# Softmax blocks on VectorE in batches of three instead of two, and seven query chunks in the first of two layers

## The chip, the cores and the metric

The kernel runs on one core of one Trainium2 chip. The metric is the device time of one execution in microseconds (us). A core has five engines with instruction queues of their own: TensorE (PE in the profile, its weight loads PEld), VectorE (DVE), ScalarE (ACT), GpSimd (POOL) and SyncE (SP, which here issues DMAs). They run beside each other and meet at semaphores. SBUF is the on-chip memory; PSUM, eight banks of 512 fp32 columns, is where matmuls write.

## The reference

Two rounds of attention and a gated MLP over 2048 tokens of width 512, with the same weights in both rounds:

```python
x = A_x
x = x + _A_ref(_layernorm(x), A_wq, A_wk, A_wv, A_wo)
x = x + _B_ref(_layernorm(x), B_w_in, B_w_sp, B_b_sp, B_w_out)
x = x + _A_ref(_layernorm(x), A_wq, A_wk, A_wv, A_wo)
x = x + _B_ref(_layernorm(x), B_w_in, B_w_sp, B_b_sp, B_w_out)

def _A_ref(x, wq, wk, wv, wo):          # H = 32 heads of Dh = 16, one shared key and value head
    q = (x @ wq).reshape(B, S, H, Dh).transpose(0, 2, 1, 3)
    k, v = x @ wk, x @ wv
    scores = einsum('bhqd,bkd->bhqk', q, k) * Dh ** -0.5
    p = softmax(scores, axis=-1)
    return einsum('bhqk,bkd->bhqd', p, v).transpose(0, 2, 1, 3).reshape(B, S, H * Dh) @ wo

def _B_ref(x, w_in, w_sp, b_sp, w_out):
    z = gelu(x @ w_in)                  # 1792 wide, two halves of 896
    z1, z2 = z[..., :896], layernorm(z[..., 896:])
    g = einsum('ts,bsf->btf', w_sp, z2) + b_sp[None, :, None]   # mixes over all 2048 tokens
    return (z1 * g) @ w_out
```

The bulk of the work is the softmax: 2 layers x 32 heads x 2048 queries x 2048 keys are exponentiated.

## The kernel before

**Blocks, units, groups, chunks.** A *block* is the scores of 128 keys by 512 query columns, one PSUM bank. The keys are kept transposed in `kT`, in two masked versions `v`, with four copies of the key head on four row groups `j`; `qs` holds 128 rows (eight heads) of 512 query columns. One matmul of 32 rows (L1774, `_qk`) makes one block. Four blocks, one for each `j`, make a *unit* (one tile of 128 keys), and 16 units, all keys, make a *group*. Each layer has 32 groups, 512 units and 2048 blocks. Queries are cut into *chunks* (L441, `self.chunks`). For a chunk of 512 queries, the 512 columns are one set of eight heads; for one of 256, two sets stand side by side (`ns = 512 // n` in `layer_groups`), so a chunk of 256 needs only two token tiles of queries and takes four groups instead of eight. `make_q` (L808) makes the query columns.

**Exponentials.** `FillStream` fills five banks with scores, as a ring of three and a ring of two. `ExpStream` (L1434) lets ScalarE exponentiate three or two banks in one instruction into slots of `Pa` (15 slots of 512 columns). `DexStream` takes single blocks away from ScalarE and gives them to VectorE: such a block goes to a side bank of PSUM, and VectorE works it off without a table. L1626 scales it out of PSUM into fp32 `ey` (one instruction for each block). Then L1651, L1653, L1654, L1655 and L1657, each over a whole batch of `NDB` blocks, evaluate a polynomial in fp16 and add it into the bits of a bf16 number in slots of `Pd` (`NPD` slots). `LOOK` is how many units ahead of the filling such a block is picked. `PVStream` (L1517) multiplies the blocks of each unit, in order, by the values `V` (with a column of ones for the softmax sums), and so frees the slots.

**What follows a group and a chunk.** `finish_group` copies the sums out of PSUM (L841 to `oT`), transposes them (by DMA, or on PE near the end of a layer) and divides (L856, L868). After a chunk's last group, `project` multiplies by `wo` (L948) and adds to `X`, and `mixer_chunk` does the layer norm and the matmuls of `w_in` (L980 for z2, L1016 for z1). The gelu waits for a whole batch of chunks (`self.gelus`, L443), so that ScalarE changes its table of functions seldom. `spatial` (L1158, L1171, L1172) mixes over tokens for those tokens that are ready (`self.passes`, L442, names the chunk after which a pass may start), and `closing` does the last token tile, the product with z1 and `w_out` (L1217, L1228 to L1250).

**What sets the order.** Each engine runs a list that is fixed before the launch. A planner in the kernel (`Sched`) lays out all operations with assumed lengths and priorities, and writes for each engine its order with the semaphore waits it needs. So a changed constant moves work in every list. `WarmStream` (L1755) adds matmuls of a zero tile: where the planner sees fewer than `TICK_COLS + WARM` columns in 3.41 us, it puts one in, to keep PE's clock up; they compute nothing that is used.

**Loads at the start.** `load` fetches the eight parts of `A_x` and the weights, and sends `w_sp` through 16 DMA transposes into `gp` as staging (L597) and out to a scratch in HBM (L599). They share SP's queue with the transposes of the attention.

Of the kernel before, what the change touches and what calls it, by code (L numbers as in the profile page):

```python
# [370 lines left out]
E_A = 0.9657950762942451  # L371
E_C = -6.696623932488385 * E_X * E_X
E_D = 127.0 * 128.0 - E_BIAS + 128.0 * 0.43426538197757353
NDB = 2

LOOK = 6
SLACK = 0.0
AHEAD = 0.0
NEAR = 4
URGENT = 1.0  # L380
RUSH = 0.3
BACKLOG = 3.0
WARM = 1200.0
ENDX = 6
PR_LAST = 0.3
PR_SMALL = 0.6
NQS = 4
NPA = 15
NPD = 8
NWS = 16  # L390


# [37 lines left out]
class Kern:  # L430
    def __init__(self, nc, A_x, A_wq, A_wk, A_wv, A_wo, B_x, B_w_in, B_w_sp, B_b_sp, B_w_out, out):
# [6 lines left out]
        self.NT = S // P  # L438
        self.out = out
        self.w_in_d, self.w_sp_d, self.w_out_d = B_w_in, B_w_sp, B_w_out  # L440
        self.chunks = [[512, 512, 512, 256, 128, 128]] * 2  # L441
        self.passes = [[(0, 8, 1), (8, 12, 2), (12, 15, 4)]] * 2  # L442
        self.gelus = [[(0, 1), (2,), (3, 4), (5,)]] * 2  # L443
        self.s_fin = 15
        self.rings = {"full": [(0, 3), (3, 2)], "ramp": [(1, 3), (1, 3)], "pair": [(1, 2), (3, 2)]}
        self.pvb2 = 0
# [34 lines left out]
        self.Pa = sb([P, NPA, 512], BF16, "Pa")  # L481
        self.Pd = sb([P, NPD, 512], BF16, "Pd")
        nb = 512 * NDB
        E = sb([P, max(6 * nb, NF * (D + 640))], BF16, "E")
# [62 lines left out]
    def sb(self, shape, dtype, name):  # L547
        self.nsb += 1
        return self.es.enter_context(self.nc.sbuf_tensor(f"{name}_{self.nsb}", list(shape), dtype))
# [982 lines left out]
class DexStream:  # L1532
# [7 lines left out]
    def __init__(self, k):  # L1540
# [5 lines left out]
        self.open = []  # L1546
        self.owner = [None] * NPD
        self.end = [None, None]
# [13 lines left out]
    def take(self, t, js):  # L1562
# [3 lines left out]
        if self.hold or sc.bank_free() > t:  # L1566
            return None
        base = NDB * (self.nb % (NPD // NDB))
        if any(o.start is None and o.ready is not None and o.ready <= t for o in k.early_first):
# [4 lines left out]
        if not self.batch:  # L1574
# [4 lines left out]
            if backlog > BACKLOG:  # L1579
                return None  # L1580
            for i in range(NDB):
                w = self.owner[base + i]
# [7 lines left out]
        layer = k.units[fu].grp.layer  # L1590
        u = max(self.u, fu + LOOK)
        while u < len(k.units):
# [19 lines left out]
        if not self.batch:  # L1612
            self.ops = []
            self.s = self.nb % 2
            self.base = base
            self.war = [w.pv for w in self.owner[base:base + NDB] if w is not None]
            self.nb += 1
# [14 lines left out]
    def after(self, c):  # L1632
        self.ops.append(c)
        if len(self.batch) == NDB:
            self.flush()
# [76 lines left out]
class WarmStream:  # L1712
# [10 lines left out]
    def peek(self, f):  # L1723
# [7 lines left out]
        near = u < len(k.units) and (k.units[u].first or k.units[u].last)  # L1731
        t = sc.below(f, TICK_COLS + WARM + (AHEAD if near else 0.0))
        if u >= len(k.units) or k.units[u].first:
# [93 lines left out]
```

The softmax here doesn't subtract the row's maximum and nothing guards it: scores larger than these inputs give would overflow.

## Time and profile before

Three runs took 1811.81, 1813.90 and 1814.57 us, the median is 1813.9. The profiled execution has a span of 1813.8 us and a mean granted PE clock of 0.992 of full speed.

| stage, us | what runs | ACT busy | DVE busy | PE busy |
|---|---|---|---|---|
| 0 to 16 | loads, layer norm, first keys and queries | 7.49 | 13.35 | 12.81 |
| 16 to 45 | attention begins, remaining keys | 27.17 | 25.33 | 25.13 |
| 45 to 510 | attention, first layer, chunks 0 and 1 | 462.00 | 454.78 | 389.19 |
| 510 to 865 | attention with token mixing beside it | 351.59 | 325.17 | 321.54 |
| 865 to 940 | end of layer 1, keys of layer 2 | 48.06 | 73.44 | 67.63 |
| 940 to 1400 | attention, second layer | 458.78 | 448.21 | 388.50 |
| 1400 to 1761 | attention with token mixing beside it | 358.60 | 333.60 | 326.48 |
| 1761 to 1814 | closing | 18.98 | 46.85 | 47.98 |

The profile gives each engine's busy time, groups of equal instructions with their count, total and mean length, and who waited for whom. The printed length of an instruction runs from its start to its end, and instructions of one engine overlap a little in their pipeline, so the distance between two starts is what an instruction costs. The chain of waits is followed back from the last instruction: at each step to what released it.

### The profile page before, as it was taken

What the parts mean: (1) busy time and instruction counts of PE and PEld (TensorE: products, weight loads), DVE (VectorE), ACT (ScalarE), POOL (GpSimd) and SP (SyncE); (2) the same over time, 40 slices, a digit from 0 to 9 for tenths busy, and PEclk for the clock granted to TensorE, in tenths of its full rate; (3) what the DMA queues carried; (4) which work ended last, traced back from release to release, by engine and by line L of the source; (5) the groups of instructions that cost most, each with busy time, mean ns of one, the idle gap of its engine ahead of it and who ended that gap; (6) DMA issues with size and microseconds to landing.
All of it is one profiled execution on the core that took longest, in us unless ns stands there. A gap on an engine that the chain in (4) does not pass through costs nothing.

```text
span 1813.8 us, 29897 instructions
## 1 busy us (share of the span) xinstructions
PE 1579.3 (87%) x11647; PEld 463.8 (26%) x11730; DVE 1720.7 (95%) x2962; ACT 1732.7 (96%) x1561; POOL 48.5 (3%) x90
## 2 busy tenths in 40 slices
PE   8888888888889998898998888888888899989988
PEld 3222222222222222222432222222222222222334
DVE  8999999999999999987999999999999999999888
ACT  7999999999999999999589999999999999999983
POOL 2000000000000000000110000000000000000000
PEclk9999999999999999999999999999999999999999
DMA  5344110010010121121210001000110111212213
GB/s 158 100 113 103 35 27 7 7 30 18 16 47 28 29 53 47 36 59 57 52 44 7 7 7 19 18 7 4 30 24 13 44 30 30 47 28 52 65 57 113
DMA packets 154517, 75.65 MB, mean 42 GB/s; under 512 B 108548, under 2 KB 150792, under 8 KB 154376
## 3 DMA queue, kind: packets, MB, share of 16 engines
q1 hardware_dynamic: 152792, 73.56, 15.7%
q8 instruction: 94, 1.54, 0.4%
q14 instruction: 47, 0.39, 0.1%
q10 hardware_dynamic: 1584, 0.16, 0.1%
HBM read 30.97 MB, written 17.83 MB: 27 GB/s over the span
## 4 chain that ended last, share of the span: by engine, by line
ACT 43%; DVE 23%; issue 17%; PE 16%; DMA 1%; POOL 0%; ACTq 0%; POOLq 0%
ACT Pa L1434 41%; PE ps_all L1774 5%; DVE E L1626 3%; PE ps_all L1517 3%; PE ps_all L1158 3%; DVE Pd L1657 3%; DVE E L1653 2%; DVE st L641 2%; DVE E L1651 2%; DVE E L1655 2%; PE ps_all L1250 2%; PE ps_all L1755 1%; DVE gp L1171 1%; DVE E L1654 1%; DVE xn L656 1%
## 5 line engine op out<-in xcount | busy, mean ns | idle before, releaser
L1434 ACT ACTIVATE Pa<-ps_all 128x1024 bf16<-128x1024 f32 (+1 forms) x1430 | 1619.8, 1377 | 19.3 <-PE ps_all L1774 17.4
L1774 PE MATMUL ps_all<-qs,kT 32*128 32x512 bf16 x4096 | 566.5, 386 | 185.6 <-ACT Pa L1434 172.4
L1626 DVE TENSOR_SCALAR E<-ps_all 128x512 f32<-128x512 f32 x532 | 362.1, 684 | 23.3 <-PE ps_all L1774 20.5
L1755 PE MATMUL ps_all<-zero 128*128 128x512 bf16 x1066 | 326.8, 392 | 15.6 <-ACT z1s L1047 3.1
L1774 PEld LDWEIGHTS ps_all<-qs,kT 32*128 32x128 bf16 x4096 | 139.7, 91 | 766.4 <-ACT Pa L1434 725.8
L1657 DVE SCALAR_TENSOR_TENSOR Pd<-E 128x1024 uint16<-128x1024 f32 x267 | 324.2, 1214 | 4.3
L1517 PE MATMUL ps_all<-Pa,V 128*32 128x512 bf16 x3564 | 323.7, 387 | 1.6 <-DVE oT L841 1.6
L1158 PE MATMUL ps_all<-wsT,z2n 128*128 128x512 bf16 x674 | 192.8, 382 | 8.5 <-issue 3.8
L1653 DVE TENSOR_TENSOR E<-E 128x1024 f16<-128x1024 f16 x267 | 182.7, 684 | 4.7
L1517 PE MATMUL ps_all<-Pd,V 128*32 128x512 bf16 x532 | 186.1, 386 | 0.0
L1655 DVE TENSOR_TENSOR E<-E 128x1024 f16<-128x1024 f16 x267 | 182.3, 683 | 3.6
L1651 DVE TENSOR_SCALAR E<-E 128x1024 f16<-128x1024 uint16 x267 | 182.3, 683 | 1.6
L1755 PEld LDWEIGHTS ps_all<-zero 128*128 128x128 bf16 x1066 | 79.9, 98 | 182.1 <-issue 124.1
L1654 DVE TENSOR_SCALAR E<-E 128x1024 f16<-128x1024 f16 x267 | 111.6, 418 | 2.1
L1517 PEld LDWEIGHTS ps_all<-Pa,V 128*32 128x32 bf16 x3564 | 64.6, 94 | 123.2 <-issue 112.7
L1171 DVE TENSOR_TENSOR gp<-ps_all,gp 128x512 f16<-128x512 f32 x112 | 75.1, 686 | 19.0 <-PE ps_all L1158 19.0
L1158 PEld LDWEIGHTS ps_all<-wsT,z2n 128*128 128x128 bf16 x714 | 55.3, 98 | 92.0 <-issue 47.7
L980 PE MATMUL ps_all<-w_in_r,xnTB 128*128 128x448 bf16 x256 | 62.1, 355 | 2.2 <-DMA xnTB<-xn 0.7
L1016 PE MATMUL ps_all<-xnTB,w_in_r 128*128 128x512 bf16 (+2 forms) x336 | 62.5, 310 | 1.5 <-DVE z1s L1027 1.0
L1250 PE MATMUL ps_all<-E 128*128 128x512 bf16 x214 | 52.8, 380 | 4.9 <-DVE E L1235 4.0
L841 DVE CAST oT<-ps_all 128x512 bf16<-128x512 f32 x64 | 43.8, 684 | 1.3 <-PE ps_all L1517 1.2
L645 POOL TENSOR_SCALAR ve<-mv 128x2 f32<-128x2 f32 (+1 forms) x28 | 7.8, 277 | 1384.3 <-DVE mv L643 1384.1
(87 smaller groups left out, 915.4 us busy)
## 6 DMA issues: line engine op xcount, KB each, us to landing
wsT_scratch<-gp SPq DMA_DIRECT2D x16, 512.0 KB, 3.6
wsT<-wsT_scratch SPq DMA_DIRECT2D x8, 1024.0 KB, 5.4
z1s<-z_scratch SPq DMA_DIRECT2D x16, 448.0 KB, 3.7
wsT<-wsT_scratch SPq DMA_DIRECT2D x8, 512.0 KB, 3.8
z_scratch<-z1s SPq DMA_DIRECT2D x4, 896.0 KB, 5.7
X<-in_A_x_dram SPq DMA_DIRECT2D x8, 256.0 KB, 5.6
out_dram<-X SPq DMA_DIRECT2D x16, 128.0 KB, 2.1
w_in_r<-in_B_w_in_dram SPq DMA_DIRECT2D x1, 1792.0 KB, 10.2
```

The lines of the kernel that those rows point to most:

```text
L1158: ins = e.matmul(self.b32(b), self.z2n[:, s, f * 128:(f + 1) * 128], w_[:, s - s0, :] if s - s0 < na or not spare else wsp[:, s - s0 - na, :],
L1171: return e.tensor_tensor(dst, self.b32(b), dst, ALU.add)
L1434: return e.activation(k.Pa[:, base:base + n, :], k.b32(b0, n).rearrange("p (k q) -> p k q", k=n), ACTF.Exp, scale=SCALE)
L1517: ins = e.matmul(k.b32(u.grp.pvb)[32 * j:32 * j + 32, :], k.V[:, u.kt, 32 * j:32 * j + 32], b.slot, tile_position=(0, 32 * j), start=u.fir ...
L1626: c = k.sc.op("dve", lambda e: e.tensor_scalar(k.ey[:, s, 512 * i:512 * (i + 1)], k.b32(j.bank.idx)[:, 0:512], E_LOG2, E_BIAS, op0=ALU.mul ...
L1651: o2 = sc.op("dve", lambda e: e.tensor_scalar(x, lo, E_X * 2.0 ** -16, E_X * E_A, op0=ALU.mult, op1=ALU.add), d_sb(n, 0.521e-3), self.ops ...
L1653: o3 = sc.op("dve", lambda e: e.tensor_tensor(w, x, x, ALU.mult), d_sb(n, 0.521e-3), [o2, self.wfree], pr)
L1654: o4 = sc.op("dve", lambda e: e.tensor_scalar(w, w, E_C, None, op0=ALU.add), d_sb(n, 0.26e-3), [o3], pr)
L1655: o5 = sc.op("dve", lambda e: e.tensor_tensor(w, w, x, ALU.mult), d_sb(n, 0.521e-3), [o4], pr)
L1657: o7 = sc.op("dve", lambda e: e.scalar_tensor_tensor(po.bitcast(U16), y, E_D, w, op0=ALU.add, op1=ALU.add), d_sb(n, 1.042e-3), [o5] + self ...
L1755: return e.matmul(k.b32(pvb if b is None else b.idx), k.zero[:], k.zero[:, None, :].to_broadcast([P, 4, P]), start=b is not None, stop=b i ...
L1774: return e.matmul(self.b32(bank), self.kT[32 * j:32 * j + 32, g.v, kt * 128:(kt + 1) * 128], self.qs[32 * j:32 * j + 32, g.q.slot, :], til ...
```

## The change

In the first layer the 2048 queries are cut into seven chunks, 256, 256, 512, 512, 256, 128 and 128, instead of six, so that the first scores need the queries of two token tiles only; passes and gelu batches are renumbered so that they lie at the same tokens. The second layer keeps its six chunks. On VectorE a batch has three blocks instead of two, so that five of its instructions serve three blocks; with that, `Pd` gets nine slots (three batches) instead of eight (four batches), the blocks are picked eight units ahead instead of six, and the buffer `E` grows with `NDB`. The planner's limit for filler matmuls rises from 1200 to 1600 columns above its base.

```diff
-NDB = 2
-
-LOOK = 6
+NDB = 3
+
+LOOK = 8
...
-WARM = 1200.0
+WARM = 1600.0
...
-NPD = 8
+NPD = 9
...
-        self.chunks = [[512, 512, 512, 256, 128, 128]] * 2
-        self.passes = [[(0, 8, 1), (8, 12, 2), (12, 15, 4)]] * 2
-        self.gelus = [[(0, 1), (2,), (3, 4), (5,)]] * 2
+        self.chunks = [[256, 256, 512, 512, 256, 128, 128], [512, 512, 512, 256, 128, 128]]
+        self.passes = [[(0, 8, 2), (8, 12, 3), (12, 15, 5)], [(0, 8, 1), (8, 12, 2), (12, 15, 4)]]
+        self.gelus = [[(0, 1, 2), (3,), (4, 5), (6,)], [(0, 1), (2,), (3, 4), (5,)]]
```

## The prediction

> **What bounds the kernel now.** I read the busy shares first, then the stages, then the chain of waits, then single rows of the timelines.
>
> The page's first part and the busy table by stage (us; PE, PEld, DVE, ACT, POOL, then clock, DMA share, GB/s):
>
> ```profile
> PE 1579.3 (87%) x11647; PEld 463.8 (26%) x11730; DVE 1720.7 (95%) x2962; ACT 1732.7 (96%) x1561; POOL 48.5 (3%) x90
> ...
> 45.00:510.00 465.00, 389.19 (x2952) 101.37 (x2952) 454.78 (x730) 462.00 (x404) 3.74 (x8) 1.00 0.19 45
> ...
> 865.00:940.00 75.00, 67.63 (x503) 31.26 (x510) 73.44 (x188) 48.06 (x69) 9.28 (x18) 1.00 0.24 58
> ...
> 1761.00:1814.00 53.00, 47.98 (x274) 23.33 (x277) 46.85 (x112) 18.98 (x38) 1.10 (x2) 1.00 0.33 97
> ```
>
> ACT and DVE are both nearly full, so the shares alone don't say which one leads. From 45 to 510 us ACT is idle 3.0 us of 465 and DVE 10.2. ACT is idle for long only at the start, at the change of layer (865 to 940 us: 27 of 75) and after its last exponential at 1761 us. The chain of waits names the leader in the steady part (start, us, what):
>
> ```profile
> 1095.13 3.52 ACT Pa L1434 x3
> 1099.65 1.85 ACT Pa L1434 x2
> 1104.18 1.84 ACT Pa L1434 x2
> 1108.70 2.68 ACT Pa L1434 x2
> 1113.22 1.84 ACT Pa L1434 x2
> ```
>
> It comes back every 4.52 us: two exponentials over three banks and two over two, ten blocks, 2.26 us for five. The groups give the split:
>
> ```profile
> L1434 ACT ACTIVATE Pa<-ps_all 128x1536 bf16<-128x1536 f32 x704 | 1118.7, 1589 | 19.0 <-PE ps_all L1774 17.4
> L1434 ACT ACTIVATE Pa<-ps_all 128x1024 bf16<-128x1024 f32 x726 | 839.7, 1172 | 0.2
> ```
>
> One more block adds 1589 - 1172 = 417 ns. With 2.26 us for a pair, a three-bank exponential takes (2.26 + 0.417)/2 = 1.34 us of ACT's time and a two-bank one 0.92; the printed durations are longer because they overlap. ACT waits 17.4 us in all for scores. So the end is set by how many blocks ACT must do, when it starts, and a few stalls. DVE matters through the number of blocks it takes off ACT: 532 of 4096.
>
> DVE does two blocks in one turn of seven instructions. Their starts in the timeline give the true prices:
>
> ```profile
> 328.81 1.23 DVE L1657 SCALAR_TENSOR_TENSOR Pd<-E 128x1024 uint16<-128x1024 f32 x1
> 329.96 0.68 DVE L1651 TENSOR_SCALAR E<-E 128x1024 f16<-128x1024 uint16 x1
> 330.67 0.69 DVE L1653 TENSOR_TENSOR E<-E 128x1024 f16<-128x1024 f16 x1
> 331.28 0.68 DVE L1626 TENSOR_SCALAR E<-ps_all 128x512 f32<-128x512 f32 x1
> 331.88 0.42 DVE L1654 TENSOR_SCALAR E<-E 128x1024 f16<-128x1024 f16 x1
> 332.22 0.68 DVE L1626 TENSOR_SCALAR E<-ps_all 128x512 f32<-128x512 f32 x1
> 332.82 0.68 DVE L1655 TENSOR_TENSOR E<-E 128x1024 f16<-128x1024 f16 x1
> 333.53 1.22 DVE L1657 SCALAR_TENSOR_TENSOR Pd<-E 128x1024 uint16<-128x1024 f32 x1
> ```
>
> A turn is 333.53 - 328.81 = 4.72 us, 2.36 us a block. Where the next instruction reads what the last one wrote (L1651 to L1653, L1655 to L1657) the step is 0.71 us, otherwise 0.61.
>
> Last, the clock. It fell to half six times (windows near 22, 373, 840, 1271, 1415 and 1634 us). One case, PE then ACT:
>
> ```profile
> 373.01 3.17 PE L1755 MATMUL ps_all<-zero 128*128 128x512 bf16 x7
> ...
> 376.66 54.34 ACT L1434 ACTIVATE Pa<-ps_all 128x1536 bf16<-128x1536 f32 x48 [2.10 <-PE ps_all L1774]
> ```
>
> Seven filler matmuls, now at half speed, stand in PE's order ahead of the scores, and ACT waits 2.10 us. At the six places ACT's waits for scores are 1.22, 2.10, 0.38 + 1.19, 1.18, 0.18 and 0.34 + 0.50: 7.1 us together.
>
> **What the Trainium skill says.** "VectorE: DVE Perf Modes", section "The TRN2 errata", says VectorE pays a fixed cost per instruction, so one large tile pays it once and small ones each time. The trace agrees: from 512 to 1024 columns the middle steps go from 426 to 685 ns, not to the double. "TensorE: Matmul & The Clock Gate", section "What's actually happening", says the clock is half or full, decided by activity in free-running windows of about 3.4 us. The trace agrees with two levels: five-microsecond windows around three of the dips read 0.66 or 0.67, which is 3.4 us at half and the rest at full. That the window runs free of the program means a low margin can fail anywhere; the trace shows dips with no large gap before them (373, 1271 us).
>
> **The change part by part.** Counts are from the two programs' instruction orders.
>
> *Batches of three.* Turns go from 265 of two and 2 of one to 180 of three, 1 of two and 4 of one. A turn of three costs 4.72 plus a third L1626 (0.60), 0.26 for each of L1651, L1653, L1655 (685 - 426 ns), 0.13 for L1654 (half of that) and 0.54 for L1657 (1219 - 682 ns): 6.77 us, 2.26 a block. DVE then takes 546 blocks instead of 532: 546 x 2.26 = 1234 us against 532 x 2.36 = 1256, so 22 us less work on DVE although it does 14 more blocks. That 22 us is not on the path; it is slack for the next item.
>
> *Blocks moved off ACT.* ACT has 702 three-bank and 723 two-bank exponentials instead of 704 and 726: 2 x 1.34 + 3 x 0.92 = **5.4 us** on the path, 4.5 of it in the first layer. The Pd matmuls on PE (532 to 546) replace as many Pa ones: nothing.
>
> *Look-ahead 8, nine slots.* Three batches in flight instead of four, begun two units earlier. A unit lasts about 4 x 0.45 = 1.8 us, so 3.6 us more lead for a turn that is 2.05 us longer plus the wait for a third block. I cost it at nothing; PE's Pd matmuls waited 0.0 us before.
>
> *Seven chunks.* The first queries now need token tiles 0 and 1, not 0 to 3. Before, ACT's first exponential is at 15.79 us, behind the copy of xnTA for tiles 2 and 3, the query matmuls from 13.11 and the copy to qs at 14.21. In the new order PE does the wv matmuls (end 9.4 us in the old trace), one transposition (10.1), twelve query matmuls of 256 (12 x 0.107 = 1.3, to 11.4), another transposition (tile 3's xn is ready at 10.9) and four more query matmuls: the scores can start at 12.2 us, and the exponential 0.44 us later as before, at 12.65: 3.1 us earlier. After it ACT still has copies that it did earlier before (V 0.28, kT 0.47): **2.4 us** net. Key tiles come in time: two give eight blocks, 3.6 us of ACT, and the second pair's kT was written at 13.3. The chunk's further costs lie beside ACT: 16 normalisations of 0.20 us for 8 of 0.33 on DVE, 0.6 us, out of the slack above; twice as many query and z1 matmuls of half the length on PE. The new transposes of the first chunk stand in SP's queue between w_sp loads, and z1 needs the last w_sp store: it is issued after the seventh group (198 us before), and z1 starts behind 515 score matmuls, which in the old trace is at 217 us. Some twenty microseconds of margin: nothing.
>
> *WARM 1600.* 175 more filler matmuls, about 0.21 us each at full clock, 37 us on an engine that is idle 76 us of the 465. Good side: some of the 7.1 us of clock stalls. Bounds 0 and 7.1; I take **3.0**, a bit under half, as the threshold is met more safely but one filler in a bad window also delays the scores. Bad side: fillers directly ahead of a score matmul go from 450 to 503; if a tenth of these 53 costs ACT its 0.21 us, 1 us; at most 11.
>
> *Sum:* 5.4 + 2.4 + 3.0 - 1.0 = 9.8; 1813.9 - 9.8 = **1804 us**. The transition (865 to 940 us) and the tail keep their work, PE and DVE lead there, and I leave them alone.
>
> **The rivals.** *Only the moved blocks count (0.22).* The early start is lost because the ramp is then short of keys (DVE busy 25.3 of 29 us from 16 to 45) and the dips stay: 1813.9 - 5.4 = 1808.5. For it: a queue of key tiles that comes no faster. Against: the keys lead the blocks by several us.
>
> *Nothing (0.10).* Fillers cost 6 to 10 us in front of scores and eat the sum: 1813. For it: ACT waits for PE already, not the reverse, in the 17.4 us. Against: PE waits 172 us for ACT in front of scores.
>
> *Slower (0.14).* A turn of three has an L1657 of 1.7 us instead of 1.15. Evictions queued behind it on DVE (L1626, oT, gp, z1s) hold their PSUM bank longer; PE's next score group with a DVE block needs that bank, and ACT waits for the group. If one of four turns costs ACT the extra 0.54 us: 180 x 0.54 / 4 = 24 us, less the 9.8: 1828. Three batches in flight for four would work the same way, through PV and Pa's 15 slots. Against: DVE's order is laid out with these lengths.
>
> **How the numbers follow.** 0.54 for the forecast, 0.22, 0.10, 0.14 for the rivals. Faster by over 0.2%: 0.54 + 0.22 = 0.76; within: 0.10; slower: 0.14. Low end: all clock stalls gone and no cost of fillers, 1813.9 - 5.4 - 2.4 - 7.1 = 1799, less 2 for DVE's own slack: 1797. High end 1813 leaves out the slower case and some of the one before.
>
> **What would show it.** Right: first exponential near 12.7 us; a turn near 6.8 us in DVE's timeline; ACT's busy time about 5 us less; fewer than six dips; ACT's wait for scores below 17.4 us. Wrong: ACT waiting for PE over 25 us; PE's Pd matmuls waiting for L1657; ACT idle again before 45 us for more than 3 us.

## The result, and the profile after

The changed kernel took 1802.5 us (median of four runs, 1800.9 to 1808.6), the kernel before 1813.3: a ratio of 0.9947, 95% interval 0.9923 to 0.9971. Predicted were 1804.

The busy shares and the four groups that matter here, from the page of the changed kernel (group: busy us, mean ns, idle before and its releaser):

```profile
PE 1604.6 (89%) x11861; PEld 480.7 (27%) x11949; DVE 1699.9 (94%) x2576; ACT 1725.3 (96%) x1556; POOL 56.2 (3%) x90
...
L1434 ACT ACTIVATE Pa<-ps_all 128x1536 bf16<-128x1536 f32 (+1 forms) x1425 | 1612.7, 1391 | 13.7 <-PE ps_all L1774 11.7
L1774 PE MATMUL ps_all<-qs,kT 32*128 32x512 bf16 x4096 | 560.1, 385 | 154.1 <-ACT Pa L1434 140.1
L1626 DVE TENSOR_SCALAR E<-ps_all 128x512 f32<-128x512 f32 x546 | 368.7, 681 | 27.1 <-PE ps_all L1774 25.2
L1755 PE MATMUL ps_all<-zero 128*128 128x512 bf16 x1241 | 374.3, 386 | 13.4 <-DVE st L1071 3.7
```

Five exponentials fewer, 7.1 us less of them (1619.8 before). DVE is busy 20.8 us less although it does 14 blocks more. ACT's waits for scores went from 17.4 to 11.7 us; 0.8 us of waits for slots of `Pa` came in beside them.

A turn of three in DVE's timeline, and ACT's start:

```profile
332.11 1.76 DVE L1657 SCALAR_TENSOR_TENSOR Pd<-E 128x1536 uint16<-128x1536 f32 x1
333.79 0.95 DVE L1651 TENSOR_SCALAR E<-E 128x1536 f16<-128x1536 uint16 x1
334.77 0.96 DVE L1653 TENSOR_TENSOR E<-E 128x1536 f16<-128x1536 f16 x1
335.65 1.28 DVE L1626 TENSOR_SCALAR E<-ps_all 128x512 f32<-128x512 f32 x2
336.85 0.55 DVE L1654 TENSOR_SCALAR E<-E 128x1536 f16<-128x1536 f16 x1
337.38 0.69 DVE L1626 TENSOR_SCALAR E<-ps_all 128x512 f32<-128x512 f32 x1
337.99 0.95 DVE L1655 TENSOR_TENSOR E<-E 128x1536 f16<-128x1536 f16 x1
338.97 1.76 DVE L1657 SCALAR_TENSOR_TENSOR Pd<-E 128x1536 uint16<-128x1536 f32 x1
```

```profile
12.35 6.89 ACT L1434 ACTIVATE Pa<-ps_all 128x1536 bf16<-128x1536 f32 x6 [0.17 <-PE ps_all L1774]
...
20.48 0.28 ACT L728 ACTIVATE V<-ps_all 128x128 bf16<-128x128 f32 x1 [0.75 <-DVE kT L723]
...
21.16 40.07 ACT L1434 ACTIVATE Pa<-ps_all 128x1536 bf16<-128x1536 f32 x35
```

338.97 - 332.11 = 6.86 us for three blocks, 2.29 each, where two took 4.72. The first exponential starts 3.44 us earlier than at 15.79.

The clock, in the two profiled runs: half speed for 27.3 us in all before, for 3.4 us after, in one dip near 244 us. There ACT has the only two waits between 44 and 447 us that its timeline shows:

```profile
244.96 1.02 ACT L1434 ACTIVATE Pa<-ps_all 128x1024 bf16<-128x1024 f32 x1 [0.46 <-PE ps_all L1774]
247.03 13.73 ACT L1434 ACTIVATE Pa<-ps_all 128x1536 bf16<-128x1536 f32 x12 [1.05 <-PE ps_all L1774]
```

**Where the time came from.** Read at three points of both traces: the last exponential of the first layer ends at 853.8 us for 864.8 before (-11.0), that of the second at 1749.1 for 1761.4 (-12.3), the span ends at 1800.1 for 1813.8 (-13.7; the profiled run of before took 1815.6 us, over its median, and its clock was among the lowest). So four fifths of it arise in the first layer. There the first exponential comes 3.4 us earlier; the exponentials, counted from start to start, take 5.4 us less (ten blocks fewer on ACT are 4.5 of that); ACT's waits for scores and slots behind the first exponential are 3.2 us shorter (7.4 to 4.2). Against that stand 1.2 us of copies that now come after the first exponential and of the 0.75 us wait at 20.48 us. Together that is 10.8 us. From there to the last exponential only 1.3 us are gained, where two blocks (0.9) and shorter waits (10.0 to 8.1) would give 2.8: the change of layer, from the last exponential of one layer to the first of the next, takes 38.2 us for 35.9, with 57 token-mixing matmuls (L1158) left over behind the layer's last values matmul for 32. The closing gives 1.4.

### The profile page after: what moved, and what is told of

The parts are those of the page before. It is cut to its first block, busy times and chain, and to the rows that moved or that the text cites. A ratio compares the mean times of both kernels' runs of the same rounds, so it can differ in the third digit from the quotient of the medians.

```text
span 1800.1 us, 29924 instructions
## 1 busy us (share of the span) xinstructions
PE 1604.6 (89%) x11861; PEld 480.7 (27%) x11949; DVE 1699.9 (94%) x2576; ACT 1725.3 (96%) x1556; POOL 56.2 (3%) x90
## 4 chain that ended last, share of the span: by engine, by line
ACT 45%; DVE 19%; PE 18%; issue 17%; POOL 1%; DMA 0%; ACTq 0%; POOLq 0%; DVEq 0%
ACT Pa L1434 43%; PE ps_all L1774 5%; PE ps_all L1517 3%; DVE E L1626 3%; PE ps_all L1158 3%; DVE Pd L1657 3%; PE ps_all L1250 2%; PE ps_all L1755 2%; DVE E L1653 1%; DVE E L1655 1%; DVE E L1651 1%; DVE st L641 1%; DVE st L1071 1%; PE ps_all L980 1%; DVE gp L1171 1%
## 5 line engine op out<-in xcount | busy, mean ns | idle before, releaser
L1434 ACT ACTIVATE Pa<-ps_all 128x1536 bf16<-128x1536 f32 (+1 forms) x1425 | 1612.7, 1391 | 13.7 <-PE ps_all L1774 11.7
L1774 PE MATMUL ps_all<-qs,kT 32*128 32x512 bf16 x4096 | 560.1, 385 | 154.1 <-ACT Pa L1434 140.1
L1626 DVE TENSOR_SCALAR E<-ps_all 128x512 f32<-128x512 f32 x546 | 368.7, 681 | 27.1 <-PE ps_all L1774 25.2
L1755 PE MATMUL ps_all<-zero 128*128 128x512 bf16 x1241 | 374.3, 386 | 13.4 <-DVE st L1071 3.7
L1517 PE MATMUL ps_all<-Pa,V 128*32 128x512 bf16 x3550 | 322.1, 385 | 0.9 <-DVE oT L841 0.9
L1657 DVE SCALAR_TENSOR_TENSOR Pd<-E 128x1536 uint16<-128x1536 f32 (+2 forms) x185 | 319.0, 1724 | 2.3
L1158 PE MATMUL ps_all<-wsT,z2n 128*128 128x512 bf16 x668 | 188.4, 382 | 8.7 <-issue 3.9
L1517 PE MATMUL ps_all<-Pd,V 128*32 128x512 bf16 x546 | 187.0, 386 | 0.0
L1655 DVE TENSOR_TENSOR E<-E 128x1536 f16<-128x1536 f16 (+2 forms) x185 | 173.3, 937 | 2.0
L1653 DVE TENSOR_TENSOR E<-E 128x1536 f16<-128x1536 f16 (+2 forms) x185 | 173.2, 936 | 2.0
L1651 DVE TENSOR_SCALAR E<-E 128x1536 f16<-128x1536 uint16 (+2 forms) x185 | 173.1, 936 | 1.4
L1755 PEld LDWEIGHTS ps_all<-zero 128*128 128x128 bf16 x1241 | 92.1, 97 | 203.6 <-issue 145.2
L1654 DVE TENSOR_SCALAR E<-E 128x1536 f16<-128x1536 f16 (+2 forms) x185 | 100.4, 543 | 0.8
L1517 PEld LDWEIGHTS ps_all<-Pa,V 128*32 128x32 bf16 x3550 | 64.7, 94 | 120.9 <-issue 113.6
L1158 PEld LDWEIGHTS ps_all<-wsT,z2n 128*128 128x128 bf16 x714 | 56.6, 98 | 88.5 <-issue 43.6
L1016 PE MATMUL ps_all<-xnTB,w_in_r 128*128 128x512 bf16 (+2 forms) x364 | 63.0, 299 | 1.1 <-DVE z1s L1027 0.6
L1250 PE MATMUL ps_all<-E 128*128 128x512 bf16 x214 | 52.2, 380 | 4.1 <-DVE E L1235 2.6
```

The lines of the kernel that those rows point to most:

```text
L1158: ins = e.matmul(self.b32(b), self.z2n[:, s, f * 128:(f + 1) * 128], w_[:, s - s0, :] if s - s0 < na or not spare else wsp[:, s - s0 - na, :],
L1434: return e.activation(k.Pa[:, base:base + n, :], k.b32(b0, n).rearrange("p (k q) -> p k q", k=n), ACTF.Exp, scale=SCALE)
L1517: ins = e.matmul(k.b32(u.grp.pvb)[32 * j:32 * j + 32, :], k.V[:, u.kt, 32 * j:32 * j + 32], b.slot, tile_position=(0, 32 * j), start=u.fir ...
L1626: c = k.sc.op("dve", lambda e: e.tensor_scalar(k.ey[:, s, 512 * i:512 * (i + 1)], k.b32(j.bank.idx)[:, 0:512], E_LOG2, E_BIAS, op0=ALU.mul ...
L1651: o2 = sc.op("dve", lambda e: e.tensor_scalar(x, lo, E_X * 2.0 ** -16, E_X * E_A, op0=ALU.mult, op1=ALU.add), d_sb(n, 0.521e-3), self.ops ...
L1653: o3 = sc.op("dve", lambda e: e.tensor_tensor(w, x, x, ALU.mult), d_sb(n, 0.521e-3), [o2, self.wfree], pr)
```

## The experiments

### Each part alone

Beside the three kernels of this part, and beside the first of the next, the kernel before took 1813.1 us (median). Where one clock is given for a kernel, it is that of its profiled run; "half clock" is time in which PE's granted clock was half.

```diff
-WARM = 1200.0
+WARM = 1600.0
```

> The kernel before with WARM 1600 alone (1258 filler matmuls for 1066, one block fewer on VectorE). Theory A, three separate gains (blocks moved 5.4 us, earlier start 2 to 3 us, clock stalls 3 to 7 us): 1807 to 1811 us, the clock up from 0.992 to 0.998 or more. Theory B, nearly all of the gain is the clock: 1803 to 1805 us. Theory C, fillers are harmless but useless and the batch of three carries the gain: 1813 us.

1812.8 us, ratio 0.9998 (0.9990 to 1.0006): nothing. Its profiled run had the clock at 0.998, with ACT's waits for scores at 11.4 us, as in the changed kernel, and took 1809.7. But its 13 runs had clocks from 0.994 to 0.999, median 0.997, for 0.995 in the kernel before: the dips became fewer and didn't go. None of the three theories; C gives the right time, but the clock is better. A second profiled run of it:

> A second look at WARM 1600 alone, for another pair of time and clock. Theory D: if the time is near the median of 1812.8, the clock is 0.993 to 0.996; if the clock is 0.998 or more, the time is below 1810.5. Rival E', fillers cost what the clock gives: 1812 to 1814 us at a clock of 0.998.

1811.1 us at a clock of 0.999, between the two ranges. The time of this kernel does fall with its clock, as D had it: over the 13 runs from 1815.6 us at 0.994 to between 1809.7 and 1811.6 at 0.998. But runs of the kernel before that happened to have a clock of 0.997 or 0.998 took 1810.5 to 1811.7 us too. So what the better clock gave, the plan with the added fillers took back for the most part.

```diff
-NDB = 2
-LOOK = 6
+NDB = 3
+LOOK = 8
...
-NPD = 8
+NPD = 9
```

> The kernel before with batches of three, LOOK 8 and nine slots alone: 549 blocks on VectorE for 532, chunks and fillers' limit as before. Theory A: 17 blocks fewer on ScalarE, about 7 us less, 1806 to 1808 us with the old clock stalls (0.992 to 0.995). Theory B: 1811 to 1814 us. Theory C: 1803 to 1805 us.

1819.5 us, ratio 1.0047 (1.0032 to 1.0062; the ratio counts the run of 1828.1 us in, by the medians it is 6.4 us): slower, which no theory had. A second profiled run:

> A second look at batches of three alone, whose first profiled run (1828.1 us, 47.8 us of half clock) was 9 us above its median. Theory D, about 0.3 us for each us of half clock over a plan that is itself 3 to 6 us slower at the end: near 1819.5 us with 18 to 30 us of half clock and a tail near 57 us. Rival E, the clock has nothing to do with it: 1819 us with as little half clock as the kernel before had, 27 us, and ScalarE's waits for scores no longer than its 17.4 us.

1820.2 us, with 30.7 us of half clock, little more than the profiled run of before had (27.3): near what theory D had. Its tail, from the last exponential to the end, is 57.3 us for 52.4, as much as the whole difference between the two profiled runs (4.6). PE's timeline behind the last L1517 shows why:

```profile
1772.69 1.73 PE L1016 MATMUL ps_all<-xnTB,w_in_r 128*128 128x128 bf16 x28
1774.47 1.67 PE L1158 MATMUL ps_all<-wsT,z2n 128*128 128x512 bf16 x7
1775.98 0.60 PE L1217 MATMUL ps_all<-z2n 128*128 128x256 bf16 x4
1776.42 0.81 PE L1158 MATMUL ps_all<-wsT,z2n 128*128 128x512 bf16 x3
1777.07 1.26 PE L1217 MATMUL ps_all<-z2n 128*128 128x256 bf16 x10
1778.16 0.59 PE L1158 MATMUL ps_all<-wsT,z2n 128*128 128x512 bf16 x2
...
1808.40 0.81 PE L1158 MATMUL ps_all<-wsT,z2n 128*128 128x512 bf16 x3
1809.04 6.21 PE L1250 MATMUL ps_all<-E 128*128 128x512 bf16 x28
```

In the kernel before, L1016 is followed by L1217 directly:

```profile
1773.15 1.73 PE L1016 MATMUL ps_all<-xnTB,w_in_r 128*128 128x128 bf16 x28
1776.22 1.70 PE L1217 MATMUL ps_all<-z2n 128*128 128x256 bf16 x14 [1.34 <-DVE z2n L1081]
```

Here token-mixing matmuls (L1158) are left over among the closing's L1217 and L1250. Some 61 come after the last values matmul, for 32, and the last three at 1808.40 us, ahead of the last L1250; in the kernel before the last one ends 10 us behind the last exponential. In the first layer, eight blocks fewer on ACT (3.6 us) end it only 0.9 us earlier, since ACT waited there 10.0 us for 7.4.

```diff
-        self.chunks = [[512, 512, 512, 256, 128, 128]] * 2
+        self.chunks = [[256, 256, 512, 512, 256, 128, 128], [512, 512, 512, 256, 128, 128]]
...
```

> The kernel before with seven chunks in the first layer alone: 528 blocks on VectorE for 532. Theory A: 3.4 us earlier first exponential less 4 blocks of 0.45 us: 1811 to 1813 us. Theories B and C: 1813 to 1816 us.

1813.4 us, 0.9998 (0.9991 to 1.0005). The first exponential is at 12.51 us, and still the first layer ends at 864.7, as before. Its exponentials take 1.9 us more (VectorE takes four blocks fewer there), ACT's waits for scores are as long as they were (7.4), and one more wait uses up most of the rest of the 3.3 us: ACT's copy of `V` at 25.38 us, which waits for VectorE's copy of keys (L723):

```profile
25.38 0.28 ACT L728 ACTIVATE V<-ps_all 128x128 bf16<-128x128 f32 x1 [1.20 <-DVE kT L723]
```

That is the prediction's first rival in small, a start that comes before the keys do. In the times as measured, the early start alone left nothing.

### Each part taken out of the changed kernel

```diff
-WARM = 1600.0
+WARM = 1200.0
```

> The changed kernel with WARM back at 1200 (1056 fillers for 1241; 546 blocks on VectorE as in it). Theory A: 3 to 7 us slower than the changed kernel, 1805 to 1810 us, with dips of the clock back (0.992 to 0.996). Theory B: 1811 to 1814 us. Theory C: 1802 to 1804 us.

1808.7 us, 0.9977 (0.9965 to 0.9988), with 30.7 us of half clock: theory A. Without the added fillers about half of the gain is gone.

```diff
-        self.chunks = [[256, 256, 512, 512, 256, 128, 128], [512, 512, 512, 256, 128, 128]]
+        self.chunks = [[512, 512, 512, 256, 128, 128]] * 2
...
```

> Batches of three with WARM 1600, six chunks (546 blocks on VectorE, 1243 fillers). From the profiled runs so far each us of half clock cost about 0.3 us. Theory D, batch alone was slow because its plan leaves PE short of work and the clock falls (47.8 us of half clock): with the fillers 1805 to 1809 us, clock 0.997 or more. Rival E, batch alone was slow because token-mixing matmuls were left over for after the last exponential (66 at the end for 32), whatever the clock: 1811 to 1817 us.

1808.5 us, 0.9967 (0.9955 to 0.9980); the kernel before took 1813.4 beside this kernel and the next. The time is theory D's, the reason only in part: the profiled run had a clock of 0.998, but the five runs had 0.995 in the median, as the kernel before, for 0.994 in batches alone. Beside batches alone, the fillers bring 11 us by the medians, of which the clock can be 3 at most (at the 0.27 us for a us at half clock that is worked out below). The rest is another plan: in the two profiled runs the first layer ends at 854.4 us for 863.9, ACT's waits there are 2.1 us for 10.0 (fewer dips count in here), 45 token-mixing matmuls for 61 are left over at the end, and the tail is 52.9 us for 57.3. So rival E's leftover was part of it, though its time was wrong.

```diff
-NDB = 3
-LOOK = 8
+NDB = 2
+LOOK = 6
...
-NPD = 9
+NPD = 8
```

> Seven chunks with WARM 1600, batches of two (525 blocks on VectorE, 7 fewer than before; 1226 fillers). Theory D: the start 3.3 us earlier, 3.2 us more of blocks on ScalarE, the clock stalls mostly gone: 1806 to 1810 us, clock 0.997 or more. Rival E', fillers alone bring nothing whatever else is there: 1812 to 1814 us.

1808.9 us, 0.9974 (0.9964 to 0.9984), clock 0.997 in the profiled run and 0.998 in the median of nine: D, not E'.

The eight cases side by side (us from 1813.3, by the ratios):

| | batches of two | batches of three |
|---|---|---|
| six chunks, WARM 1200 | 0 | +8.5 |
| six chunks, WARM 1600 | -0.4 | -6.0 |
| seven chunks, WARM 1200 | -0.4 | -4.2 |
| seven chunks, WARM 1600 | -4.7 | -9.6 |

Beside the two others, chunks are worth 3.6 us, batches 4.9 and fillers 5.4, each give or take some 5 by the intervals, so that the first isn't clear of nothing. From the kernel before, none gains anything.

**The clock taken out.** Each run has a mean clock, which gives its time at half clock: twice the missing share of the clock, times the run. One slope was fitted to the 166 runs of the twelve kernels of this document, with a level for each kernel: a us at half clock costs 0.27 us (0.25 to 0.29). The kernel before spent 21 us a run at half clock on average (71 runs), 5.6 us of its time, the changed kernel 10, 2.7 us. The levels are the times at full clock, an estimate good to 0.4 to 0.8 us. From the kernel before (1808.3):

| at full clock | batches of two | batches of three |
|---|---|---|
| six chunks, WARM 1200 | 0 | +5.4 |
| six chunks, WARM 1600 | +1.2 | -4.7 |
| seven chunks, WARM 1200 | -1.3 | -5.8 |
| seven chunks, WARM 1600 | -0.9 | -7.4 |

So of the gain some 3 us are clock and some 7 the plan of the other work. Batches of three are what gains at full clock, but only with one of the other two parts: alone they get a plan that is 5 us slower than the kernel before, with either other part one that is 5 to 6 us faster, and with both about 2 more. The added fillers, beyond what the clock gives, make four differences between these kernels: +1.2, +0.4, -1.6 and, with batches of three and six chunks, -10.1 us.

### The constants of the changed kernel

The kernel before measured 1813.4 us beside WARM 2000 and 1814.8 beside the other three.

```diff
-WARM = 1600.0
+WARM = 2000.0
```

> The changed kernel with WARM 2000. Theory D: no half-clock time is left, so the slowest runs of the changed kernel (1808.6 at clock 0.993) disappear; the fillers delay scores somewhat: 1800 to 1804 us with a spread under 3 us. Rival: more fillers stand in front of scores, 1806 to 1812 us at full clock.

1805.9 us (1805.8 to 1806.7), 0.9957 (0.9945 to 0.9969), clock 0.999. The spread is under 1 us, as D had it, but the time is nearer the rival's range, 4.0 us over the changed kernel's profiled run at the same clock (1801.9), for 219 fillers more. That would be 18 ns each if nothing else of the plan counted. But other things count: VectorE takes four blocks fewer in the first layer (ACT's exponentials there take 2.4 us more), and the tail is 1.2 us longer, while ACT's waits for scores and slots in that layer fall (3.1 us for 4.4). So this is no price of a filler.

```diff
-WARM = 1600.0
+WARM = 1700.0
```

> The changed kernel with WARM 1700: 548 blocks on VectorE, 1339 fillers (98 more), 33 leftover matmuls at the end of layer 1 for 52, 41 at the end of layer 2 for 31. Theory F: blocks 0.9 us less, fillers 1.8 us more, leftover 4.1 less and 2.2 more: 1800 to 1804 us. Rival: fillers alone set the difference between WARM 1600 and 2000, so a quarter of 3.4 us: 1803 to 1804 us with the same end of layer 1.

1810.1 us, 0.9976 (0.9967 to 0.9984): both theories missed. In the profiled run the clock is full all the time. The tail is 55.2 us for 51.0, with 66 token-mixing matmuls left over for 30; ten more had been counted, at 2.2 us. The first layer takes 3.9 us longer, and ACT's timeline has most of it: VectorE takes four blocks fewer there (ACT's exponentials take 2.1 us more), the planner gives ACT three copies of z2 (L993, 1.8 us, and 0.8 of waiting for them), and the waits for scores and slots are 1.1 us shorter. So a step of 100 in one constant moves the plan by as much as a whole part of the change.

```diff
-LOOK = 8
+LOOK = 9
```

> The changed kernel with LOOK 9: VectorE takes 532 blocks as in the kernel before, in batches of three; 1240 fillers; 25 token-mixing matmuls between the last values matmul of layer 1 and the closing instead of 52. Theory F, the time is ScalarE's blocks plus what is left over at the layer's end: 14 more blocks on ScalarE, 6 us slower, and 27 matmuls of 0.215 us fewer in the way, up to 5.8 us faster: 1803 to 1807 us. Rival G, blocks on ScalarE hardly count and the leftover does: 1797 to 1801 us. Rival H, only the blocks count: 1807 to 1810 us.

1810.1 us, 0.9976 (0.9966 to 0.9985), 5.3 us slower than the changed kernel by the ratios: at the edge of the range of rival H, that only the blocks count. VectorE has 11 blocks less in the first layer, and it ends 4.4 us later in the profiled run. That is 0.40 us for a block, close to the 0.417 of the prediction. Behind that the leftover does count: with 24 token-mixing matmuls for 57 the change of layer takes 2.2 us less (36.0 for 38.2). But the second layer takes 3.5 us more, with only 3 blocks less on VectorE, and the tail, with 43 matmuls left over for 30, 2.0 us more.

```diff
-LOOK = 8
+LOOK = 6
```

> The changed kernel with LOOK 6 as before the change: 552 blocks on VectorE (6 more), 1342 fillers (101 more), 43 leftover matmuls for 52. Theory F with the cost of fillers seen between WARM 1600 and 2000 (about 18 ns each at full clock): 2.6 us less for the blocks, 1.9 less for the leftover, 1.8 more for fillers: 1799 to 1802 us. Rival I, the longer turn of a batch of three needs the longer lead: values matmuls wait for L1657, and ScalarE's wait for scores rises over 25 us: 1806 to 1815 us.

1835.4 us, 1.0122 (1.0109 to 1.0136): rival I, and far beyond it. In the table of waits of this kernel the wait that stands out is one that was 0.8 us in the changed kernel (us in total, times, longest):

```profile
ACT Pa L1434 <- PE ps_all L1517: 23.9, 24, 2.9
ACT E L1229 <- PE ps_all L1217: 22.6, 13, 4.5
ACT Pa L1434 <- PE ps_all L1774: 15.3, 26, 3.8
PEld ps_all L1517 <- DVE Pd L1657: 13.7, 38, 1.4
```

The second row is in every kernel here. The first and the last fit one chain: the values matmul stands in PE's order and waits for VectorE's last instruction of a turn (13.7 us; 0.7 in the changed kernel), so the slots of `Pa` aren't freed, and ACT waits for slots with its scores ready. The clock is at 0.998.

## Why the prediction was right

**The turn of three** was to cost 6.77 us and cost 6.86; DVE's busy time fell 20.8 us where 22 were worked out.

**Blocks moved off ACT:** 5.4 us predicted; the group's busy time fell 7.1, and LOOK 9, which gives those blocks back, costs 0.40 us a block in the first layer. At full clock LOOK 9 is 7.7 us slower than the changed kernel; its 14 blocks would be 5.8 at the prediction's price.

**Seven chunks:** the first exponential was to come at 12.65 us and came at 12.35. The copies that follow it on ACT were counted as 0.7 us of loss; copies and the wait for the keys took 1.2. Net that is 2.2 us, for 2.4 predicted. Taken alone, though, the earlier start was lost again in the same layer.

**Look-ahead and slots** "at nothing" holds only for the value that was chosen. With batches of three and LOOK 6, the slower rival's second way (through PV and Pa's 15 slots) is real: 33 us over the changed kernel. The prediction named the path and then gave it no price of its own.

**WARM** was put down with 3.0 us of stalls saved and 1.0 lost. The saving came out: some 11 us less of half clock a run, at 0.27 us each, are 2.9 us. The 7.1 us of stalls read from the profile were sound too: 27.3 us at that price are 7.4. The loss stays open. WARM 1600 alone costs 1.2 us at full clock, but in the changed kernel the same fillers save 1.6 there, and WARM 1700, with fewer fillers than WARM 2000, costs more (8.0 us over the changed kernel for 4.9). The price for a filler in front of scores was never seen apart from a changed plan.

**The transition and the tail, "I leave them alone":** they didn't stay. The change of layer took 2.3 us more and the tail 1.4 less, which happen to cancel nearly. In batches alone and in WARM 1700 the tail took 4.8 and 4.2 us more. In all these traces a long leftover of token mixing goes with a long change of layer (24 to 40 matmuls with 34.3 to 36.0 us, 50 to 78 with 36.8 to 42.2) and with a long tail (26 to 45 with 50.7 to 53.1 us, 61 and 66 with 55.2 to 57.3).

**What no step of it held:** that the parts are not additive. Taken singly from the kernel before, they give 0, 0 and +6 to +8 us; at full clock -1.3, +1.2 and +5.4. Each constant makes the planner lay out all lists anew, and what is then left over at a layer's end, and which windows of the clock run short, comes out differently. The sum was right for the three together: 6.8 us without the clock for 7.4, and 3.0 of clock for 2.9. That it fits so well is in part luck. WARM 1700, with two blocks more off ACT and the same early start, lies at 1810 us and at full clock 0.6 us over the kernel before; WARM 2000 at 1806 and 2.5 below it; LOOK 9 at 1810 and 0.3 over. How much of the 10.8 us is owed to this one plan among its neighbours stays open. No version tried was faster than the changed kernel.

## What to carry to other kernels

When an engine that helps out is freed by batching its instructions, its gain is the work that it takes off the leading engine, priced per block there; and the batch's longer turn must be given lead, or the consumer in its fixed order waits. Fillers can hold the clock up, and here half of the time at half clock went; but more of them was not better, and what they cost could not be told from the plan. Where the runs report a clock, fit the time against it before two kernels are compared: a profiled run may be far from the median clock. In a kernel whose lists come from a planner, test each constant of a change beside the others, not alone from the old state.

## What the runs showed of the hardware

The dips of the clock have no long pause of PE before them. I cut the trace of the kernel before into windows of 3.41 us, on the grid on which the dips begin, and added up the time in which matmuls stream (columns at 2.4 per ns, as 512 of them take when 15 such matmuls start 0.216 us apart; matmuls side by side counted once). The six windows just before a dip are filled to 0.35 to 0.43, and their longest gap is 0.7 to 1.7 us; the others are filled to 0.64 in the median, and only two of them lie below 0.43 (0.402 and 0.419). In the changed kernel the window before its one dip has 0.386, and two others lie below 0.43 (0.389, 0.427). Over the 13 traces that have a dip, 43 of the 46 windows before one are below 0.445, and 27 of some 6800 others are. So in these traces a dip goes with a window filled to less than about 0.44, but that alone doesn't settle it: dips also followed windows of 0.45, 0.50 and 0.51.

A us at half clock cost 0.27 us over the 166 runs (0.26 over the 71 of the kernel before alone), where PE is busy 87% (before) or 89% (the changed kernel) of the span. Single pairs of runs scatter more: 0.46 between the two profiled runs of batches alone.
